# Moving left-over keys and score pairs, and holding loads to four in flight, in a T5-bias attention with a maxout feed-forward

## The chip, the cores and the metric

The kernel runs on one core of one Trainium2 chip. The metric is the device time in microseconds of one execution. One launch computes everything; nothing is computed on the host.

## What is computed

Attention with a bias that depends on the distance of query and key alone, for 8 batch elements, 8 heads, 576 positions and 64 elements a head, and behind it a feed-forward layer that takes the largest of three products:

```python
scores = scale * np.matmul(q, k.transpose(0, 1, 3, 2))
scores = scores + bias.transpose(2, 0, 1)[None, :, :, :]      # bias_table[bucket(|i - j|)]
attn = np.exp(scores - max) / sum                             # softmax over keys
attn_out = np.matmul(attn, v)
x = attn_out.transpose(0, 2, 1, 3).reshape(4608, 512)
h = np.maximum(np.maximum(x @ w1, x @ w2), x @ w3)            # 512 -> 768
out = h @ w_out                                               # 768 -> 512
```

## The kernel before

**Tiling.** A *visit* `(b, hp)` is a batch index `b` (0 to 7) and a pair of heads `hp` (0 to 3). Its 576 positions are four tiles of 128 and a rest of 64, the left-over keys and queries. Scores are computed with the keys on the partitions; ScalarE takes their exponential (`exp`, line 800) into `e4` (four key tiles) and `el` (left-over keys of both heads in its first 576 columns, left-over queries behind them). The bias is a factor: VectorE multiplies the columns near the diagonal by a band (`times_band`, `times_bandt`, `times_band_left`). `attend` or `attend_rows` multiplies by `v`, whose extra column of ones gives the sums, and its `quotients` divide into `x_sb`. After a batch's last head pair SP's DMA transposes bring `x_sb` into `xT` (lines 946, 994), which the feed-forward reads.

**Stages.** Batches 0 and 1 and visit (2,0) use small portions of the feed-forward between the attention's parts (`fill`, which also calls the *hooks* that it is given between portions). In later visits a feed-forward whose matmuls use 64 rows of the array, in pairs, takes the place of the portions: the *tiled* visits, from (2,2) on, take their feed-forward from `plain_gates` and `plain_outputs`, in the order `begin0, end0, begin1, end1`; `begin` computes the first rows' half, `end` the other half. From visit (4,0) (`ROWS`) on, scores run one key tile at a time over 512 queries (`key_scores`, two matmuls), the attend is `attend_rows`, and the next visit's first key tile is already computed by `ahead` at the end of a visit. (4,0) has no visit of this form before it, so its list `begun` is empty.

**PSUM.** Scores, left-over keys (`sct`) and left-over queries (`scq`) share the pool `ps_s` with two buffers, so each needs the exponential of the last but one to be done.

**Order.** Every engine runs its instructions in the order of the program, where `inorder` asks for it. On TensorE this is nearly everything. SP issues all DMA transposes and the output stores in one order. POOL issues the loads of `q`, `k`, `v` (they cast to bf16): from batch 2 on it does nothing else.

**Loads.** In `b`'s visit `hp == 2`, `load_v(b + 1)` is issued behind a transpose of batch `b + 1` (for `b` from 4 on, the one of the last full key tile), then `load_qk(b + 2)`. These are six transfers for v (four tiles and two tails) and eleven for q and k (eight tiles, q's tail, two of k's). `load_qk(b + 2)` goes behind the same transposes for `b < 4`, behind v's last transfer (`last_v`) from `b = 4` on. All of a batch's transposes `transposes(b + 1)`, five pairs of q and k with the tails last, are issued during visits `hp` 1 and 2 of batch `b`. A dependence of this sort is a semaphore wait on POOL, added by `go_behind`.

**Lines that the steps touch.** `in_turn` (147) wraps each load; `keys_first` (1192) sets the order of the score groups of visits (2,0) and (3,0); lines 1194 to 1200 begin a rows visit; 1245 is its third key tile; 1272 to 1284 are the tiled visit with the left-over keys of (3,0); 1323 and 1330 issue the loads; 1340 to 1344 end a visit that isn't tiled, with the left-over keys of (2,0) behind the hooks.

Of the kernel before, what the change touches and what calls it, by code (L numbers as in the profile page):

```python
# [39 lines left out]
def kernel(  # L40
# [21 lines left out]
    QM = 2 * QS  # L62
    KT = 4
    ROWS = (4, 0)
    FCH = d_ff // P
    DCH = d_model // P
    NTOK = B * S
# [76 lines left out]
    def tail_part(src, b, h0, h1, par):  # L144
        return src[b, h0 + par : h1 : 2, KT * P : S, :].rearrange("h p d -> p h d")

    def in_turn(b, load):
        return inorder(load)

    def load_main(src, b, h0, h1, dst, t0=0, t1=KT):  # L150
        x = main_part(src, b)
# [45 lines left out]
    def load_v(b, h0, h1, behind=None):  # L197
        loads = load_main(v, b, h0, h1, vx[b % 2][:, :, :, 0:D]) + load_tail(v, b, h0, h1, v_diag)
        go_behind(loads, behind)
        return loads[-1]  # L200
# [972 lines left out]
    for b, hp in [(b, hp) for b in range(1, B) for hp in range(HP)]:  # L1173
        if hp == 0:
            x_sb[b] = x_tile()
        qT, kT = (x[:, hp, :] for x in qk[b])
        e4, el = begun[0] if begun else e_tiles()
        together = b > 1 and (b, hp) != (2, 0)
        tiled = bool(stages)
        rows = (b, hp) >= ROWS  # L1180
        if (b, hp) == ROWS:
            free_banks()
            ps_a, ps_f = banks(1)
            pending.clear()
            thirds = [after]
        rate = 8 if b == 1 or (b, hp) == (2, 0) else 13

        if tiled:  # L1190
            run, after = stages.pop(0)
        keys_first = hp == 0 and b in (2, 3)
        order = [(0, 0), (1, 0), (0, 2), (1, 2)] if keys_first else [(0, 0), (0, 2), (1, 0), (1, 2)]
        if rows:
            if not begun:
                key_scores(qT, kT, e4, 0)
            begun.clear()
            end_sums = late.pop(0)()
            key_scores(qT, kT, e4, 1)
            quotients = end_sums()  # L1200
        else:
            for c, tt in order[:2]:
                scores(qT, kT, e4, c, tt)
        store_outputs()
        if b == 1:
            if hp == 0:
                crossbar = transposes(2)
            next(crossbar, None)
        elif hp and b + 1 < B:
            if hp == 1:  # L1210
                crossbar = transposes(b + 1)
            for _ in range((KT + 1, 2, KT + 1)[min(b, 4) - 2]):
                next(crossbar, None)
        early()
        if turned:
            turned.pop(0)()
        if not rows:
            quotients = next_late()
        if not tiled or rows:
            times_band(hp, e4, 0, 0, QS, inorder)  # L1220
        quotients()
        if rows:
            times_band(hp, e4, 1, 0, QM, inorder)
        if b == 1 and hp + 1 < HP:
            spread_packed(hp + 1, nc.vector)
        if (b, hp) == (1, 1):
            add_ffn(QS, QS)

        def keys():
            sums_first = together and (not tiled or len(pending) < 2)  # L1230
            if sums_first:
                next_late()()
            if (b, hp) != (3, 0):
                left_keys(hp, qT, kT, el, 0, S)
            if together and not sums_first:
                next_late()()

        if rows:
            begin2, end2 = thirds.pop()()
            if not run.keys_late:  # L1240
                end_keys = left_keys_rows(qT, kT, el)
            begin2()
            if not run.keys_late:
                end_keys()
            key_scores(qT, kT, e4, 2)
            largest = end2(2 if run.keys_late else 1)

            def bands():
                times_band(hp, e4, 2, 0, QM, inorder)
                times_bandt(hp, el)  # L1250
                times_band(hp, e4, 3, 0, QM, inorder)

            def left():
                left_queries(hp, qT, kT, el)
                times_band_left(hp, el)

            def ahead():
                n = HP * b + hp + 1
                if n < HP * B:
                    begun.append(e_tiles())  # L1260
                    key_scores(*(x[:, n % HP, :] for x in qk[n // HP]), begun[0][0], 0)

            run(
                lambda: key_scores(qT, kT, e4, 3), left, ahead, largest, bands, lambda: left_keys_rows(qT, kT, el)
            )
            thirds.append(after)
        elif tiled:
            if len(pending) > 1:
                fill(DCH)
            keys()  # L1270
            fill(FCH)
            if (b, hp) == (3, 0):
                left_keys(hp, qT, kT, el, 0, S)
            times_band(hp, e4, 0, 0, QS, inorder)
            begin0, end0, begin1, end1, alone = run
            scores(qT, kT, e4, *order[2])
            begin0()
            exp_left = left_queries(hp, qT, kT, el)
            turned_1 = begin1()
            times_band(hp, e4, 1, 0, QM, inorder)  # L1280
            band_left = times_bandt(hp, el)
            go_behind([band_left], turned_1[-1])
            times_band_left(hp, el)
            scores(qT, kT, e4, *order[3])
            dve0 = end0([exp_left])
            dve1 = end1([band_left])
            times_band(hp, e4, 2, 0, QM, inorder)
            dve0()
            times_band(hp, e4, 3, 0, QM, inorder)
            dve1()  # L1290
            pending.extend((n, [fn]) for n, fn in alone)
        else:
            late_keys = (b, hp) == (2, 0)
            fill(8 if (b, hp) == (2, 1) else rate, (lambda: None) if late_keys else keys, *([lambda: None] if together else []))
            if not late_keys:
                times_bandt(hp, el)


            def beside_scores():
                banks = [pool.tile([P, KT * 64], F32, tag=tag, name="scq") for pool, tag in ((ps_a, "a"), (ps_f, "ff"))]  # L1300
                turn_left_queries(qT, kT, banks)
                put_left_queries(el, banks)

            visit(qT, kT, e4, order[2:], None if together else beside_scores, el=el if together else None)
        store_outputs()
        if b == 1 or hp in (1, 2) and b + 1 < B:
            for _ in range(2 if b > 1 else 1):
                next(crossbar, None)
        early()
        if turned:  # L1310
            turned.pop(0)()
        if not together:
            quotients = next_late()
            times_band(hp, e4, 1, 0, QM, inorder)
            quotients()
        if b == 1 and hp + 1 < HP:
            second_transposes(qk[1], hp + 1)
        if hp == 1 and b > 1:
            pending.extend((n, [fn]) for n, fn in rest)
            rest.clear()  # L1320
            made, tail = ffn((b - 1) * CH, CH, False, [(b + (i + 2) // HP, (i + 2) % HP) >= ROWS for i in range(HP)])
        if hp == 2 and b + 1 < B:
            last_v = load_v(b + 1, 0, H, turned_qk[b + 1, 1, 1 if b < 3 else 2 if b == 3 else KT - 1])
            if b == 1:
                load_last_weights(turned_qk[2, 1, KT - 1])
                batch[3] = load_tiles()
                load_qk(3, turned_qk[2, 1, KT - 1])
        if hp == 2 and 1 < b < B - 2:
            batch[b + 2] = load_tiles()
            load_qk(b + 2, turned_qk[b + 1, 1, KT - 1] if b < 4 else last_v)  # L1330

        def queries():
            times_band(hp, e4, 3, 0, QM, inorder)

        def bands_2():
            for t in range(1 if together else 2, 3):
                times_band(hp, e4, t, 0, QM, inorder)

        if not tiled:
            fill(rate, bands_2, queries)  # L1340
            if late_keys:
                keys()
                times_bandt(hp, el)
            times_band_left(hp, el)
        if hp == 1 and b > 1:
            stages.extend(made)
            strict.append(b)
        if ROWS <= divmod(HP * b + hp + 1, HP) < (B, 0):
            late.append(lambda b=b, hp=hp, e4=e4, el=el: attend_rows(b, hp, e4, el))
            continue  # L1350
        for half in range(2):
            late.append(lambda b=b, hp=hp, e4=e4, el=el, half=half: attend(b, hp, e4, el, half))
# [50 lines left out]
```

## Time and profile before

| | us |
|---|---|
| median of 3 runs | 312.46 (311.75 to 313.81) |
| the profiled execution, whole | 312.09 |
| its span on the core | 310.3 |
| TensorE busy | 296.2 |
| ScalarE busy | 202.0 |
| VectorE busy | 206.9 |
| visits (4,0) to (7,3), about | 122 to 252 |

The page counts an engine as busy while an instruction of it is under way; the rest of its span it waited or had nothing to do. Busy shares by slice of the span, in tenths (40 slices of 7.76 us), and the share of the 16 DMA engines:

```profile
PE   8889989999998999999999999989999999999995
...
DVE  6487878777775767676777677765777665553552
ACT  3999978977767677868776877775777730122221
POOL 8977660962087104930429032832300000000000
...
DMA  9999999999999999999699999999932113202003
```

The transfers keep the DMA engines occupied until about 235 us. By queue:

```profile
q0 software_dynamic: 103840, 16.66, 78.3%
q1 hardware_dynamic: 58304, 22.69, 44.7%
q8 instruction: 35, 0.57, 0.8%
```

The columns are packets, MB and the time the packets took, as a share of 16 engines' span. `q0` are POOL's loads, `q1` what SP issues, `q8` the engines' instructions.

### The profile page before, as it was taken

How to read it: one execution, taken by the hardware profiler on the slowest of the kernel's cores; microseconds unless marked ns; L12 is line 12 of the kernel's file. 1: busy time of each engine (PE TensorE's matmuls, PEld its weight loads, DVE VectorE, ACT ScalarE, POOL GpSimd, SP SyncE). 2: the span in 40 equal slices, each digit the busy share in tenths (PEclk: the TensorE clock that was granted, in tenths of full speed). 3: DMA queues.
4: the chain of work that ended last, by engine and by line, in shares of the span. 5: the costliest groups of instructions: out<-in, count | busy, mean ns of one | idle time of the engine just before them, and what ended most of it. 6: DMA issues, size and time to landing. Idle time of an engine off the chain costs nothing.

```text
span 310.3 us, 10531 instructions
## 1 busy us (share of the span) xinstructions
PE 296.2 (95%) x4534; PEld 182.3 (59%) x4547; DVE 206.9 (67%) x471; ACT 202.0 (65%) x273; POOL 110.6 (36%) x147
## 2 busy tenths in 40 slices
PE   8889989999998999999999999989999999999995
PEld 2357867765554655667666666666667654444442
DVE  6487878777775767676777677765777665553552
ACT  3999978977767677868776877775777730122221
POOL 8977660962087104930429032832300000000000
PEclk9999999999999999999999999999999999999999
DMA  9999999999999999999699999999932113202003
GB/s 166 179 197 198 181 166 142 100 163 133 141 137 223 145 183 157 122 135 139 152 169 104 139 114 225 131 135 172 176 63 106 37 19 93 101 0 104 34 0 135
DMA packets 163950, 40.48 MB, mean 130 GB/s; under 512 B 153784, under 2 KB 159424, under 8 KB 163904
## 3 DMA queue, kind: packets, MB, share of 16 engines
q0 software_dynamic: 103840, 16.66, 78.3%
q1 hardware_dynamic: 58304, 22.69, 44.7%
q8 instruction: 35, 0.57, 0.8%
q10 hardware_dynamic: 1760, 0.47, 0.7%
q14 instruction: 11, 0.09, 0.1%
HBM read 35.39 MB, written 9.45 MB: 144 GB/s over the span
## 4 chain that ended last, share of the span: by engine, by line
PE 74%; DMA 11%; ACT 4%; SPq 4%; DVE 2%; issue 1%; POOL 0%; POOLq 0%
PE psp L107 31%; PE ps L107 15%; PE a L107 11%; PE sc L107 7%; DMA q_sb<-in_q_dram 5%; PE pso L107 5%; SPq L711 4%; ACT e L800 4%; DMA vx<-in_v_dram 2%; DMA kT<-k_sb 2%; PE sct L107 2%; DMA kT<-ktail 2%; PE warm L107 1%; PE scq L107 1%; PE tp L111 1%
## 5 line engine op out<-in xcount | busy, mean ns | idle before, releaser
L800 ACT ACTIVATE e<-sc 128x1024 bf16<-128x1024 f32 x128 | 128.8, 1026 | 29.8 <-PE sc L107 28.6
L107 PEld LDWEIGHTS <-w_bf 64*128 64x128 bf16 (+1 forms) x1088 | 73.7, 95 | 57.5 <-issue 3.4
L107 PE MATMUL psp<-xT,w_bf 64*128 64x512 bf16 x736 | 91.2, 376 | 1.4 <-DVE e L780 1.3
L780 DVE TENSOR_TENSOR e<-e,hank 128x512 bf16<-128x512 bf16 (+2 forms) x120 | 56.4, 476 | 17.6 <-ACT e L800 17.2
L107 PE MATMUL ps<-xT,w_bf 128*128 128x512 bf16 (+1 forms) x345 | 64.7, 335 | 1.4 <-DVE k_sb L228 1.0
L153 POOL DMA_DIRECT2D vx<-in_v_dram x28 | 24.6, 897 | 73.8 <-PE scq L107 26.0
L107 PE MATMUL sc<-qT,kT 64*128 64x256 bf16 (+1 forms) x384 | 47.9, 306 | 2.3 <-ACT e L800 1.0
L107 PEld LDWEIGHTS <-kT 64*128 64x128 bf16 (+1 forms) x736 | 30.6, 94 | 28.1 <-issue 8.7
L107 PE MATMUL a<-vx,e 64*128 64x65 bf16 (+1 forms) x1536 | 44.6, 191 | 0.0
L107 PEld LDWEIGHTS <-e 64*128 64x128 bf16 (+1 forms) x1536 | 40.6, 95 | 3.8
L107 PEld LDWEIGHTS <-hT 64*128 64x128 bf16 (+1 forms) x444 | 27.2, 95 | 19.2 <-DVE hT L528 1.3
L800 ACT ACTIVATE el<-sct 128x576 bf16<-128x576 f32 (+2 forms) x36 | 21.7, 606 | 16.3 <-PE sct L107 15.1
L107 PE MATMUL a<-vt,el 64*128 64x65 bf16 (+1 forms) x240 | 30.9, 201 | 0.4 <-DVE m L488 0.4
L398 ACT ACTIVATE m<-ps 128x512 bf16<-128x512 f32 x14 | 8.4, 597 | 34.3 <-PE ps L107 34.3
L107 PEld LDWEIGHTS <-el 64*128 64x128 bf16 (+1 forms) x624 | 25.9, 95 | 8.1 <-issue 5.5
L107 PE MATMUL psp<-wo_bf,hT 64*128 64x256 bf16 (+1 forms) x336 | 29.7, 307 | 0.0
L181 POOL DMA_DIRECT2D q_sb<-in_q_dram x24 | 22.2, 926 | 15.3 <-DMA xT<-x_sb 6.8
L181 POOL DMA_DIRECT2D k_sb<-in_k_dram x24 | 22.2, 924 | 3.3 <-DMA wo_bf<-in_moe_w_out_dram 1.2
L107 PE MATMUL pso<-wo_bf,hT 128*128 128x512 bf16 (+2 forms) x103 | 22.6, 367 | 0.2
L800 ACT ACTIVATE el<-scq 128x512 bf16<-128x512 f32 (+1 forms) x38 | 19.5, 530 | 2.7 <-PE scq L107 2.6
L407 DVE TENSOR_TENSOR m<-ps,m 128x512 bf16<-128x512 f32 x14 | 9.7, 692 | 17.0 <-PE ps L107 17.0
L107 PE MATMUL sct<-qT,kT 64*128 64x288 bf16 (+3 forms) x96 | 16.7, 284 | 2.9 <-DMA kT<-ktail 1.6
(83 smaller groups left out, 291.5 us busy)
## 6 DMA issues: line engine op xcount, KB each, us to landing
out_dram<-osb SPq DMA_DIRECT2D x35, 256.0 KB, 2.8
vx<-in_v_dram POOLq DMA_DIRECT2D x28, 128.0 KB, 6.6
q_sb<-in_q_dram POOLq DMA_DIRECT2D x26, 128.0 KB, 7.6
k_sb<-in_k_dram POOLq DMA_DIRECT2D x24, 128.0 KB, 8.0
w_bf<-in_moe_w_dram POOLq DMA_DIRECT2D x3, 768.0 KB, 9.3
xT<-in_k_dram SPq DMA_DIRECT2D x6, 128.0 KB, 4.3
hank<-w_dr SPq DMA_DIRECT2D x2, 384.0 KB, 5.5
wo_bf<-in_moe_w_out_dram POOLq DMA_DIRECT2D x1, 768.0 KB, 9.0
```

Source lines behind the costliest of these rows:

```text
L107: made = inorder(nc.tensor.matmul(*args, **kw))
L111: inorder(nc.tensor.transpose(*args))
L153: in_turn(b, nc.gpsimd.dma_start(out=dst[:, t, h0:h1, :], in_=x[:, t, h0:h1, :])) for t in range(t0, t1)
L181: loads.append(in_turn(b, nc.gpsimd.dma_start(out=dst[:, t], in_=main_part(src, b)[:, t])))
L398: nc.scalar.activation(out=st[fb]["m0"][:], in_=ps0, func=ACTF.Copy)
L407: inorder(nc.vector.tensor_tensor(out=m[:], in0=ps1, in1=st[fb]["m0"][:], op=ALU.max))
L711: turned_qk[b, j, t] = inorder(nc.sync.dma_start_transpose(out=made[j][:, :, P * t : P * t + n], in_=src))
L780: put(nc.vector.tensor_tensor(out=e4[:, t, :, lo:hi], in0=e4[:, t, :, lo:hi], in1=hank[:, 2 * hp : 2 * hp + 2, c0:c1][:, :, ::-1], op=ALU. ...
L800: made = nc.scalar.activation(out=out_, in_=in_, func=ACTF.Exp, scale=inv_sqrt_d)
```

## The change

Four edits, which leave the number of matmuls, activations, vector operations and transfers as it is.

1. Left-over keys. In (3,0) `left_keys` moves from ahead of the third score group to behind `begin1`. In (2,0) `keys()` and its `times_bandt` move from the end into the first hook of the last `fill`, ahead of the bands of tiles 1 to 3; and (2,0) takes its score groups in the usual order.
2. (4,0) computes the scores of key tiles 0 and 1 ahead of the attend of (3,3), and of tile 2 in its middle, where it computed tile 0 ahead, tile 1 in the middle and tile 2 after the left-over keys. The later visits, which find a begun tile, stay as they were.
3. From batch index 5 on, each load waits until the load four before it has landed. Batch 5's first four have none before them. The wait stands on POOL's queue.
4. `load_qk(b + 2)` goes behind the key transpose for all `b`, no longer behind v's last transfer: it concerns batches 6 and 7.

```diff
+    PACED, DEEP = 5, 4
...
+    in_flight = []
+
     def in_turn(b, load):
-        return inorder(load)
+        load = inorder(load)
+        if b >= PACED:
+            if len(in_flight) >= DEEP:
+                go_behind([load], in_flight[-DEEP])
+            in_flight.append(load)
+        return load
...
-        keys_first = hp == 0 and b in (2, 3)
+        keys_first = (b, hp) == (3, 0)
         order = [(0, 0), (1, 0), (0, 2), (1, 2)] if keys_first else [(0, 0), (0, 2), (1, 0), (1, 2)]
         if rows:
-            if not begun:
-                key_scores(qT, kT, e4, 0)
+            lead = not begun
             begun.clear()
+            for t in range(2) if lead else ():
+                key_scores(qT, kT, e4, t)
             end_sums = late.pop(0)()
-            key_scores(qT, kT, e4, 1)
+            key_scores(qT, kT, e4, 2 if lead else 1)
             quotients = end_sums()
...
-            key_scores(qT, kT, e4, 2)
+            if not lead:
+                key_scores(qT, kT, e4, 2)
...
-            if (b, hp) == (3, 0):
-                left_keys(hp, qT, kT, el, 0, S)
             times_band(hp, e4, 0, 0, QS, inorder)
             begin0, end0, begin1, end1, alone = run
             scores(qT, kT, e4, *order[2])
             begin0()
             exp_left = left_queries(hp, qT, kT, el)
             turned_1 = begin1()
+            if (b, hp) == (3, 0):
+                left_keys(hp, qT, kT, el, 0, S)
             times_band(hp, e4, 1, 0, QM, inorder)
             band_left = times_bandt(hp, el)
             go_behind([band_left], turned_1[-1])
...
-            last_v = load_v(b + 1, 0, H, turned_qk[b + 1, 1, 1 if b < 3 else 2 if b == 3 else KT - 1])
+            load_v(b + 1, 0, H, turned_qk[b + 1, 1, 1 if b < 3 else 2 if b == 3 else KT - 1])
...
-            load_qk(b + 2, turned_qk[b + 1, 1, KT - 1] if b < 4 else last_v)
+            load_qk(b + 2, turned_qk[b + 1, 1, KT - 1])
...
-            fill(rate, bands_2, queries)
-            if late_keys:
+            def late_products():
                 keys()
                 times_bandt(hp, el)
+
+            fill(rate, *([late_products] if late_keys else []), bands_2, queries)
             times_band_left(hp, el)
```

## The prediction

> **What bounds the kernel now.** I read the page first. TensorE has nearly every microsecond and its clock is full, so a change in other work is worth only what TensorE now loses to it.
>
> ```profile
> PE 296.2 (95%) x4534; PEld 182.3 (59%) x4547; DVE 206.9 (67%) x471; ACT 202.0 (65%) x273; POOL 110.6 (36%) x147
> PEclk9999999999999999999999999999999999999999
> ```
>
> The span is 310.3 us, so TensorE idles 14 us in all. About 6 us of that lie in the first 42 us and 3.4 us in the last 10, which the change doesn't touch. Then I asked TensorE's own timeline, from 42 us to the end, for every matmul with an idle time over 0.15 us before it. There are five; 0.31 and 0.21 us at 53.5 and 66.1 are small. The other three:
>
> ```profile
> 94.29 0.42 PE L107 MATMUL sct<-qT,kT 128*128 128x512 bf16 x2 [1.63 <-DMA kT<-ktail]
> ...
> 123.81 0.21 PE L107 MATMUL a<-vt,el 64*128 64x65 bf16 x2 [0.39 <-DVE m L488]
> ...
> 209.87 1.04 PE L107 MATMUL psp<-xT,w_bf 64*128 64x512 bf16 x8 [1.29 <-DVE e L780]
> ```
>
> The bracket is the idle time and what ended it. These 3.31 us, 1.1% of the span, are the whole purse. The chain of waits tells where the first comes from:
>
> ```profile
> 86.35 2.02 SPq L711
> ...
> 88.47 5.78 DMA kT<-ktail
> 94.25 0.05 issue
> 94.29 0.42 PE sct L107 x2
> ```
>
> SP issues batch 3's ten transposes one after the other; the last, of the left-over keys, goes out at 88.47 and lands at 94.25, 1.6 us after TensorE wants it for (3,0). The third gap is a puzzle: the VectorE product it names (208.79 to 209.21) isn't read by that matmul, and the bank it writes had last been read by a VectorE copy that ended at 207.34. The page's transfers, with the median time from issue to landing at the end, say the rest of what I use:
>
> ```profile
> vx<-in_v_dram POOLq DMA_DIRECT2D x28, 128.0 KB, 6.6
> q_sb<-in_q_dram POOLq DMA_DIRECT2D x26, 128.0 KB, 7.6
> k_sb<-in_k_dram POOLq DMA_DIRECT2D x24, 128.0 KB, 8.0
> ```
>
> POOL issues one load each 0.87 us and they take 7 to 8 us to land, so more than four are in flight: the limit will bind. That the change does nothing there is excluded.
>
> **What the skill says.** "Runtime: NRT & Kernel Launch", Instruction fetch mechanics: an engine's instructions arrive by DMA in blocks of 256, mostly hidden. The page's instruction queue agrees in size (35 packets, 0.57 MB: 16 KB each); one starts at 207.44, when TensorE had started 420 matmuls and weight loads since the last (196.65), and TensorE stands from 208.58 to 209.87. So I take the third gap for a late block; no page says that it can be that late. "DMA: Bandwidth & Descriptors", Queues, rings and completion order: an engine goes round-robin between queues, a packet at a time. The trace agrees as far as it shows: a transpose takes 2.4 us from issue to landing at best and 9.8 at worst, when loads are under way. "TensorEngine Tiling (Array Packing)", Key Properties: a change of tiling mode drains TensorE. Here eight 64-row scores would have ended about 89.18 by their mean spacing, and the 128-row product behind them starts at 89.27: an estimate of 0.09 us for a change.
>
> **The change, part by part.** The sum is against the profiled execution's own 312.09 us (span 310.3 and 1.8 around it); the median of the runs is 312.46, 0.37 above it.
>
> (3,0), left-over keys later. Nothing is removed: two matmuls (0.35 us until the next), one exponential (0.65) and one band product (0.26) go behind scores (0.23), the first rows of two gates (0.86 each) and the left-over queries (0.12). The order by TensorE from 92.66: scores, rows, queries, rows end at 94.73, and the transpose has landed at 94.25, so the 1.63 us go. The queries need q's tail, which went out two transposes earlier and landed at about 91.3. What is late next: ScalarE does this exponential third, not first, ending at 95.95, and VectorE's band product, on which the second pair's other rows wait, at 96.2, where TensorE would be at 96.15: 0.1 lost. The product now stands between 64-row matmuls: two more mode changes, 0.2. Net -1.3, bounds -1.63 and -0.5: the first attend of (3,1), 99.26 now, would run at 97.7, and batch 3's last v tail lands at 97.55, with no margin.
>
> (2,0), score order and left-over keys earlier. Same instructions. TensorE meets the keys at 64.0 instead of 64.94, their transpose landed at 63.41: no wait, 0.6 us margin. ScalarE's order is the same. VectorE is in order, though: the left-over keys' band product now stands ahead of bands 2 and 3, and waits for the exponential that ends at 66.03, where these bands started at 65.46. So they come 0.57 + 0.25 = 0.8 us later, band 2 at 66.85; attend's first half starts at 66.41 and meets it after two key tiles, at 66.5. +0.4 (0 to +0.8).
>
> (4,0), two score pairs first. The second pair (0.22 us) fills the gap of 0.39 before attend. But the scores have two banks: the third pair then needs the first one's exponential (ends 124.76, TensorE there at 124.56) and the keys behind it the second's (ends 125.8, there at 125.6). What is filled is paid back: 0 (-0.25 to +0.2).
>
> Loads from batch 5 on. The first four of q, k(5) go as before; the fifth waits for the first, and so on. POOL has no other work at that time, so behind its waits stand only loads. q and k(5) land 2.7 to 5.5 us before their transposes are issued; one waiting longer by up to 4 us costs little. For v, six loads, the last tail now waits for the second v tile: it landed 7.4 us after the first issue in batch 5, and a lone load lands in 3.7 to 4.0 us, so the last tail lands 11.4 us after the first issue in place of 10.4 (151.70 to 162.11); the same sum gives 10.9 against 11.0 in batch 6 and 11.5 against 10.0 in batch 7. Attend wants them at 163.09, 194.74 and 227.69, margins of 1.0, 0.0 and 2.6. The transfers before v(5) shift with TensorE by the 0.9 net gained so far, since xT's transposes start on VectorE's quotients and SP runs on from there: wanted 162.2, landed 162.2. Cost 0 (to +1.0).
>
> q and k(6), (7) directly behind v. They waited for all of v; SP then stood before their transposes: 165.1 to 166.16 and 168.4 to 169.91 in batch 6, 198.0 to 199.49 and 200.7 to 201.37 in batch 7. This 2.5 and 2.1 us go, and v(6), which waits for the last of these key transposes, is issued 2.5 us earlier: the margin of nothing at 194.74 becomes 2. TensorE gains what it lost there, about 0.15 (first attend group 0.91 against 0.75 us). Loads now run beside xT's transposes (158 to 165), which have over 3 us until the gates read them: 0.
>
> The fetch at 208. No more than four loads ahead of a block, and q, k(7) earlier: likely less, but it is one event in one execution. -0.65, bounds -1.29 and, if another block is caught elsewhere, +0.7.
>
> Sum: -1.3 + 0.4 + 0 + 0 - 0.15 - 0.65 = -1.7, so 310.4 on the profiled time and 310.8 on the median; I say 310.5.
>
> **The rivals.** First, *all gaps close*: -1.63 - 0.25 - 0.15 - 1.29 with (2,0) free is -3.3: 308.8. For it speaks that each gap has its own edit; against it the two-bank and band arithmetic above. Second, *the gain turns into waits for v*: TensorE gains 1.3 in batch 3 and gives it back at (3,1) and (5,0), where v lands on no margin, and the fetch gap stays: 312.1. Third, on the other side, *the limit starves v*: each last tail goes out a landing later. The price: 2.5 us later than computed at (5,0) is 2.5 lost, the chain through transposes to the next v doesn't recover, 2.5 again at (6,0) less 2.0 of margin is 0.5, fetch blocks and late transposes of batch 7 at most 1.0; with none of the gains, 312.1 + 4.0 = 316.1. It decides from the point where v's last tail lands more than 12.4 us after the first issue. Against it: the loads are issued 0.9 us apart and four cover 3.5 us of a lone load's 3.7.
>
> **How the numbers follow.** Under 1% this kernel's measurement hardly tells a change from none. My forecast, a gain between 0.3 and 1%, has 0.50, with 309.4 to 311.6 as its own range; all gaps close 0.24; gain given back 0.16; v starved 0.10. Faster by over 1% (under 309.3) is the first rival, 0.24; within 1% the forecast and the second, 0.66; slower 0.10. The range, 308.8 to 313.0, holds the forecast, the second rival with its spread of the runs shown (311.75 to 313.81), and half of the first.
>
> **What would show it.** In the changed profile: the 1.63 before sct in (3,0) gone, with at most 0.3 before the next attend; a wait of 0.3 to 0.5 at the first attend of (2,1) on VectorE's bands; at (4,0) 0.1 to 0.2 left and small waits on exponentials after it; SP without the waits before batches 6's and 7's first transposes; no idle TensorE before the attends of (5,0) and (6,0). I am wrong if a wait on vx or vt of 1 us or more appears there, if left-over keys in (2,0) wait for their transpose, or if issue gaps grow in number.

## The result: 310.77 us, and where the time went

| | before | changed |
|---|---|---|
| median of 8 runs, us | 312.79 (311.75 to 314.11) | 310.77 (308.73 to 311.51) |
| ratio, 95% interval | | 0.9919 (0.9894 to 0.9943) |
| profiled execution, us | 312.09 | 311.51 |
| span, us | 310.3 | 309.7 |

The change makes the kernel 0.8% faster, 2.0 us on the medians. Ratios, and means over profiles, compare undisturbed executions alone, so a ratio can differ a little from the quotient of two medians. The changed kernel's profile comes from its slowest execution, and 1.1 us of that arose before any edit acts: it waited 0.85 us for a copy at 31.4 and 0.41 us at 36.5, in stretches where the two programs do the same. So I compare the two traces by stretches. This is the page of the changed kernel; the source has grown by eight lines at this point, so lines are up to 8 higher (L711 is L719, L153 is L161):

```profile
PE 297.2 (96%) x4547; PEld 182.1 (59%) x4547; DVE 207.4 (67%) x471; ACT 202.0 (65%) x273; POOL 110.6 (36%) x147
...
L189 POOL DMA_DIRECT2D k_sb<-in_k_dram x24 | 21.6, 899 | 10.3 <-DMA vx<-in_v_dram 4.3
...
vx<-in_v_dram POOLq DMA_DIRECT2D x28, 128.0 KB, 6.3
q_sb<-in_q_dram POOLq DMA_DIRECT2D x26, 128.0 KB, 6.6
k_sb<-in_k_dram POOLq DMA_DIRECT2D x24, 128.0 KB, 7.5
```

Each group shows count, busy time, mean ns, then the idle time ahead and what ended most of it. POOL now waits 10.3 us ahead of k's loads, 4.3 of them for loads of v (3.3 in all before): the limit binds. Half of the loads of q land within 6.6 us of their issue, in place of 7.6. These are TensorE's idle times over 0.15 us between 68 us and its last attend, from its timeline:

```profile
123.58 0.21 PE L108 MATMUL a<-vt,el 64*128 64x65 bf16 x2 [0.17 <-DVE m L496]
...
158.74 1.90 PE L108 MATMUL psp<-xT,w_bf 64*128 64x512 bf16 x16 [0.54 <-issue]
...
189.27 0.23 PE L108 MATMUL a<-vx,el 64*128 64x65 bf16 x3 [0.41 <-issue]
```

The 1.63 us before `sct` are gone. The 0.39 of (4,0) became 0.17. The 1.29 us at 209.87 are gone, but two smaller gaps of the same sort have come in other places. The view ends them by "issue": nothing that it shows was waited for.

A finer ruler than the span is the moment at which VectorE starts a visit's quotients. Changed minus before, us, at the same point of the work:

```
after the quotients of      offset   step   what lies between
(1,3), at 61.80 before      +1.11           start, the same in both programs
(2,2), at 92.08             +1.34    +0.23  (2,0) to (2,2): the edit of (2,0)
(3,0), at 102.00            -0.23    -1.57  the edit of (3,0)
(3,3), at 125.90             0.00    +0.23  the edit of (4,0)
(4,3), at 157.22            -0.01    -0.01
(5,0), at 165.00            +0.70    +0.71  the gap at 158.74
(5,2), at 181.01            +0.39    -0.31
(5,3), at 188.84            +0.96    +0.57  the gap at 189.27 (ahead of this instruction)
(6,0), at 196.81            +0.80    -0.16
(6,2), at 213.98            -0.67    -1.47  the gap at 209.87 of before
end                         -0.59    +0.08
```

From (1,3) on that makes 1.7 us gained. It looks like the prediction's own sum, term by term, but the experiments show that two of these terms differ from one execution to the next. I call such a term a draw.

### The profile page after: what moved, and what is told of

It reads as the page before. It is cut to its first block, busy times and chain, and to the rows that moved or that the text cites. A ratio compares the mean times of both kernels' runs of the same rounds, so it can differ in the third digit from the quotient of the medians.

```text
span 309.7 us, 10546 instructions
## 1 busy us (share of the span) xinstructions
PE 297.2 (96%) x4547; PEld 182.1 (59%) x4547; DVE 207.4 (67%) x471; ACT 202.0 (65%) x273; POOL 110.6 (36%) x147
## 4 chain that ended last, share of the span: by engine, by line
PE 81%; DMA 9%; POOL 4%; ACT 2%; issue 2%; DVE 1%; POOLq 0%; ACTq 0%
PE psp L108 34%; PE ps L108 17%; PE a L108 12%; PE sc L108 8%; PE pso L108 6%; DMA w_bf<-in_moe_w_dram 5%; DMA xT<-in_k_dram 4%; PE sct L108 2%; POOL vx L291 2%; ACT e L808 1%; POOL q_sb L161 1%; PE scq L108 1%; DMA out_dram<-osb 1%; ACT el L808 0%; POOL vt L180 0%
## 5 line engine op out<-in xcount | busy, mean ns | idle before, releaser
L161 POOL DMA_DIRECT2D vx<-in_v_dram x28 | 24.7, 895 | 57.3 <-PE sc L108 33.1
L189 POOL DMA_DIRECT2D k_sb<-in_k_dram x24 | 21.6, 899 | 10.3 <-DMA vx<-in_v_dram 4.3
L536 DVE TENSOR_TENSOR hT<-psp,m 128x1024 bf16<-128x1024 f32 (+1 forms) x16 | 15.0, 956 | 7.3 <-PE psp L108 7.3
```

Source lines behind the costliest of these rows:

```text
L161: in_turn(b, nc.gpsimd.dma_start(out=dst[:, t, h0:h1, :], in_=x[:, t, h0:h1, :])) for t in range(t0, t1)
L189: loads.append(in_turn(b, nc.gpsimd.dma_start(out=dst[:, t], in_=main_part(src, b)[:, t])))
L536: inorder(nc.vector.tensor_tensor(out=out_[:, i : i + n], in0=ps2()[:, i : i + n], in1=m[0][:, i : i + n], op=ALU.max,))
```

## The experiments

Two theories stood at first. A: the moved keys of (3,0) carry most of the gain (my terms: -1.3 there, -0.65 for late instruction blocks). B: the limit of four carries it. Each part was made alone, then in twos.

**The left-over keys of (3,0) alone.**

```diff
-            if (b, hp) == (3, 0):
-                left_keys(hp, qT, kT, el, 0, S)
             times_band(hp, e4, 0, 0, QS, inorder)
...
             turned_1 = begin1()
+            if (b, hp) == (3, 0):
+                left_keys(hp, qT, kT, el, 0, S)
```

> The kernel before with the left-over keys of (3,0) moved alone. Theory A (the moved keys carry the gain): the idle 1.63 us before sct near 94 is gone, the first attend of (3,1) starts 1.3 to 1.6 us earlier beside the visits ahead of it, and the time is 1.0 to 1.6 us below before (ratio 0.995 to 0.997). Theory B (the load limit carries it, the gap only moves to a wait for v in (3,1)): within 0.4 us of before.

Measured: ratio 0.9969 (0.9943 to 0.9994), 1.0 us faster, with no change only just outside the interval. The wait is gone, the stretch gained 1.46 us against the profile of before. By itself that fits A.

**The edit of (2,0) alone.** `keys_first = (b, hp) == (3, 0)`, and `late_products` as the first hook.

> The kernel before with (2,0)'s score order and left-over keys changed alone. Theory A (VectorE's bands come late and the first attend of (2,1) meets them): 0.2 to 0.5 us slower between the last attend of batch 1 and (2,2), no wait for a transpose. Theory B (the keys are free there): no change of that stretch within 0.1 us. A wait for the left-over keys' transpose of 0.3 us or more would be against both.

Measured: ratio 1.0006 (0.9981 to 1.0032). The quotients of (2,0) come 0.54 us late, but at those of (2,1) 0.10 us are left, and no wait for a transpose is seen: nearly free. The profile shows more elsewhere:

```profile
97.95 0.22 PE L107 MATMUL a<-vt,el 128*128 128x130 bf16 x1 [0.69 <-DMA vt<-in_v_dram]
...
179.16 1.04 PE L107 MATMUL psp<-xT,w_bf 64*128 64x512 bf16 x8 [1.67 <-issue]
211.26 1.04 PE L107 MATMUL psp<-xT,w_bf 64*128 64x512 bf16 x8 [1.81 <-issue]
```

This kernel has the keys of (3,0) where they were, and yet no wait for their transpose; it waited for v's tail instead, at (3,1), and for 0.44 us in two parts at (5,0). And what stood once at 209.87 stands here twice, with 1.67 and 1.81 us. One profile's 1.63 and 1.29 were draws.

**The edit of (4,0) alone.** `lead`, key tiles 0 and 1 ahead, 2 in the middle.

> The kernel before with (4,0)'s two leading score pairs alone. Theory A (two banks: what is filled is paid back): the gap of 0.39 before the attend of (3,3) falls to about 0.17, but the quotients of (3,3) come 0 to 0.25 us later than before, beside the visits ahead. Theory B (filling the gap is a gain): they come 0.2 us earlier.

Measured: ratio 0.9999 (0.9974 to 1.0024). The gap before the attend fell from 0.39 to 0.17, and the quotients of (3,3) came 0.23 us later against those ahead. The same 0.23 appears in each of the three profiles with this edit, and 0.00 in those without. That is theory A: the two banks ask back more than was filled. In the changed kernel the third score pair starts at 124.58, behind an exponential that ends at 124.53, and the left-over keys at 125.50, behind one that ends at 125.45.

**Both load edits alone.** `PACED, DEEP = 5, 4`, `in_turn` as changed, and `load_qk` behind the key transpose.

> The kernel before with both load edits (four in flight from batch 5 on, q and k behind the key transpose) alone. Theory A (loads cost TensorE only at (6,0) and by late instruction blocks): 0 to 1.0 us faster, batch 5's transposes end 2 to 3 us earlier than before's 152.4, gaps in the middle of psp runs stay but shrink in sum from 1.3 to under 1.0 us. Theory B (this is the main gain): 1.3 us or more faster and no such gap at all. Starved v: waits on vx or vt of 1 us.

> The load edits alone, a second time, beside the next run. Ratio to before 0.987 to 0.993 as the first time (0.9891). In the profile the wait for the left-over keys at (3,0) is drawn anew: between 0 and 2 us.

Measured: 0.9891 (0.9856 to 0.9927), and again 0.9926 (0.9895 to 0.9956): 2.3 to 3.4 us. That is theory B's size. The left-over keys, here where they were, waited 0.49 and 0.60 us, and the gaps that remain after 130 us are one each:

```profile
93.32 0.42 PE L108 MATMUL sct<-qT,kT 128*128 128x512 bf16 x2 [0.49 <-DMA kT<-ktail]
...
207.26 1.04 PE L108 MATMUL psp<-xT,w_bf 64*128 64x512 bf16 x8 [0.17 <-issue]
```

```profile
93.70 0.42 PE L108 MATMUL sct<-qT,kT 128*128 128x512 bf16 x2 [0.60 <-DMA kT<-ktail]
...
208.01 1.04 PE L108 MATMUL psp<-xT,w_bf 64*128 64x512 bf16 x8 [0.51 <-issue]
```

Of the load edits' expectation, the end of batch 5's transposes was a half miss: 150.0 and 151.3 in these two, a gain of 1 to 2 us and not 2 to 3; in the changed kernel itself it was 152.7, no gain.

**Following alone, and the limit alone.**

```diff
-            load_qk(b + 2, turned_qk[b + 1, 1, KT - 1] if b < 4 else last_v)
+            load_qk(b + 2, turned_qk[b + 1, 1, KT - 1])
```

> The kernel before with q and k directly behind v alone, no limit of four. If following is what clears SP's waits: the waits of 1.0 and 1.5 us before the first transposes of batches 6 and 7 go, v(6) is issued 1.5 us or more earlier than 183.7, and the time is within 0.4 us of before. If following without a limit floods the transfers: transposes of batches 6 and 7 take longer from issue to landing (over 7 us in the middle) and v(6) is no earlier.

> The kernel before with the limit of four alone, q and k of batches 6 and 7 still behind v's last transfer. If the limit is what speeds the transposes up: batch 5's last key transpose lands near 149 in place of 152.4, but q and k of batch 6 start later than before, after v's slower end, and SP waits 1.5 us or more for them; time within 0.6 us of before, to either side. If following is what counts: batch 5's transposes end where they did.

Measured: following alone 0.9954 (0.9930 to 0.9979), the limit alone 0.9902 (0.9874 to 0.9930). The limit is the larger part, and it doesn't need the other edit: alone it left a gap of 0.65 at 157.53 and no more after 130 us, and batch 5's key transposes ended at 149.3. Both times were missed: following was to stay within 0.4 us of before and gained 1.4, the limit within 0.6 and gained 3.1. Why following alone gains is not shown.

The waits on SP go. Before, SP's timeline jumps from xT's transposes to the first of batch 6, and again to the second; the changed kernel's runs through, and so does that of following alone (167.66, 0.11 us behind xT):

```profile
162.51 2.56 SPq L994 DMA_TRANSPOSE xT<-x_sb  x2
166.16 2.16 SPq L711 DMA_TRANSPOSE qT<-q_sb  x1
169.91 1.19 SPq L711 DMA_TRANSPOSE kT<-k_sb  x1
```

```profile
162.47 2.56 SPq L1002 DMA_TRANSPOSE xT<-x_sb  x2
165.14 1.21 SPq L719 DMA_TRANSPOSE qT<-q_sb  x1
166.45 1.21 SPq L719 DMA_TRANSPOSE kT<-k_sb  x1
```

But the limit alone does the same, though its q and k still go behind v's last transfer:

```profile
157.98 6.33 SPq L1002 DMA_TRANSPOSE xT<-x_sb  x4
164.42 1.22 SPq L719 DMA_TRANSPOSE qT<-q_sb  x1
```

I had expected SP to wait 1.5 us or more there. With the limit alone v(5) starts at 146.38, 5.3 us earlier than before, and q and k behind it come in time. Nor does following alone bring v(6) forward: it was expected 1.5 us or more ahead of 183.7 and came at 186.18, in an execution that ran 2.0 us behind the profile of before at (5,0).

**The gaps that "issue" ends.** I took them for late blocks of TensorE's instructions. If they are, they stand where a block ends, whatever is computed there. Here TensorE's records (matmuls, weight loads and the 38 instructions of its sequencer) are counted from the start up to each such gap after 125 us, in the profiles whose records are complete (4547 matmuls, 4547 weight loads):

```
profile          instructions ahead (and modulo 256): gap, us
keys (3,0)       5571 (195): 0.11     6849 (193): 1.26
(2,0) edit       5571 (195): 1.67     6849 (193): 1.81
(4,0) edit       4033 (193): 0.31     4801 (193): 0.71    6849 (193): 2.00
changed          4801 (193): 0.54     6083 (195): 0.41
load edits       6849 (193): 0.17
```

All stand at 193 to 195 of 256. In profiles with 13 records missing, that of before among them, they stand at 185 to 187. To tell the place in the count from the place in the work, the kernel before was given 64 more TensorE instructions at its start:

```diff
-    on_zeros(warm[:, 0:CH], 9)
+    on_zeros(warm[:, 0:64], 41, 64)
```

> The kernel before with 41 narrow warming matmuls (64 columns) in place of the first 9 wide ones: 64 TensorE instructions more ahead of all the work. If the gaps in the middle of psp runs are late instruction blocks of 256: they stand again where 193 of 256 instructions have been counted (4801, 5569, 6849 and so on, counted from the start), so 64 instructions (about 2 us) earlier in the work than in the other runs, and none before the psp matmul of visit (6,3) that has the 1.29. If that matmul or its data is the cause: the gap stays before it, at 129 or so of 256 (193 + 64). Time: 0 to 6 us slower for the longer start.

Measured (the expectation names visit (6,3); it is (6,2), and its "129 or so" is a slip): two gaps, at 5561 and 6841 instructions, 185 of 256 with 14 records missing. That is the count of before (6841), and so 64 instructions earlier in the work. The second now stands before another operation:

```profile
176.60 0.61 PE L107 MATMUL psp<-xT,w_bf 64*128 64x512 bf16 x4 [1.76 <-issue]
...
209.67 0.39 PE L107 MATMUL sc<-qT,kT 64*128 64x512 bf16 x1 [2.67 <-issue]
```

Had the matmul's data been the cause, the count would have been 185 + 64 = 249 of 256. Ratio 1.0041 (1.0008 to 1.0074), with these larger gaps; a longer start isn't seen (first quotients at 19.39, before 19.37). So it is shown: TensorE stands at the ends of blocks, as its instructions come late. The packets of `q8` are TensorE's: 35 of 256 instructions make 8960, and TensorE has 9119 records. In the profile of before the block's packet starts at 207.44, 16 instructions ahead of the stop; the one before it (196.65) had started 180 ahead. From the packet's start to TensorE's next matmul 2.4 us pass, and at the ten gaps of the table 2.2 to 3.2. It is the start that is late.

The sum of these gaps after 125 us is, without the limit, 1.41 (before), 1.37, 3.48 and 4.43 us, mean 2.67; with the limit of four it is 0.95 (changed), 0.17, 0.65, 1.06, 0.51 and 2.13, mean 0.91. The limit takes away 1.8 us of late blocks by these means; they are of four and six profiles, and the largest sum with it is above the smallest without.

**Two loads in place of four.** `PACED, DEEP = 5, 2` in the changed kernel.

> The changed kernel with two loads in flight in place of four. A lone load takes 3.7 us, so two give one load each 1.9 us or more: v's last tail lands about 3 x 4 = 12 us and q and k's eleven about 22 us after their first issue. If v can be starved (the rival that ended slower): TensorE waits 1 us or more before the attends of (5,0) or (6,0) and the time is 1 to 4 us above the changed kernel. If there is slack: within 0.5 us of it.

Measured: ratio 1.0566 (1.0516 to 1.0616), 20 us slower than the changed kernel; the expectation's 1 to 4 us was far too small. It begins with the starved v of the prediction's third rival, and then the keys' transposes are late:

```profile
166.60 0.20 PE L108 MATMUL a<-vt,el 64*128 64x65 bf16 x1 [4.15 <-DMA vt<-in_v_dram]
...
198.19 0.42 PE L108 MATMUL sct<-qT,kT 64*128 64x288 bf16 x2 [3.98 <-DMA kT<-ktail]
...
207.71 0.54 PE L108 MATMUL a<-vt,el 64*128 64x65 bf16 x2 [1.62 <-DMA vt<-in_v_dram]
```

v(5)'s last tail lands 15.9 us after its first issue (151.69 to 167.58), past the 12.4 at which I had put the turning point; in the changed kernel it is 11.5 us (148.05 to 159.50). The turning point itself was too strict: with the load edits alone the tail took 12.44 us, and no attend waited, as the first issue had come at 148.19.

The waits from 160 us on sum to 15.3 us. The rest lies in TensorE's granted clock, here in tenths of full speed for 40 slices of 8.3 us:

```profile
PEclk9999999999999999999979998799989999999999
```

Four times the trace shows the granted clock at half for 3.41 us, from 167.17, 197.89, 208.13 and 238.85 on, each within 0.7 us of the end of one of the waits of 4.15, 3.98, 1.62 and 3.32 us. Half of four times 3.41 is 6.8 us, and TensorE is busy 6.6 us longer than in the changed kernel. All six executions had a mean granted clock of 0.979 or lower.

**The limit from batch 2 on**, with the load edits and the keys of (3,0).

> The left-over keys of (3,0) moved and the two load edits, with the limit of four from batch 2 on in place of 5. If crowded loads also make the late transposes and instruction blocks of batches 2 to 4: no gap over 0.2 us between 65 and 125 but the 0.39 before the attend of (3,3), and 0.3 to 1.0 us faster than the same with the limit from 5. If v or keys of batch 3 starve: waits of 0.5 us or more on vx, vt or kT there and no gain.

Measured: 1.0009 (0.9965 to 1.0052), against 0.9919 and 0.9916 for the same from batch 5 on: the 0.3 to 1.0 us that I expected on top didn't come, and the whole gain was lost. POOL's queue tells why. Ahead of `wo_bf` stands v(2)'s last tail, which now waits:

```profile
58.41 0.64 POOL L180 DMA_DIRECT2D vt<-in_v_dram  x1 [0.56 <-DMA vx<-in_v_dram]
62.74 0.61 POOL L180 DMA_DIRECT2D vt<-in_v_dram  x1 [3.71 <-DMA vx<-in_v_dram]
63.35 0.85 POOL L1065 DMA_DIRECT2D wo_bf<-in_moe_w_out_dram  x1
```

`wo_bf`, 768 KB, is issued at 63.35 in place of 58.93, and TensorE waits for it:

```profile
72.74 0.58 PE L108 MATMUL pso<-wo_bf,hT 128*128 128x512 bf16 x1 [4.21 <-DMA wo_bf<-in_moe_w_out_dram]
```

The output weights are wanted early in batch 2, and a limit there holds back a load that isn't under it. Five other profiles, where the limit didn't reach this load, waited for it too, but for 0.24 to 2.06 us. The long wait costs more than itself: around it the granted clock stood at half for 6.83 us (from 71.07 on), some 3.4 us of work, and 15 of this kernel's 18 executions had a mean granted clock of 0.995 or lower. From batch 5 on nothing else stands in POOL's queue.

**The load edits with the keys of (3,0), without (2,0) and (4,0).**

> The changed kernel without the edits of (2,0) and (4,0): left-over keys of (3,0) moved, and the two load edits. If these two cost what the trace says (0.2 each): 0.2 to 0.5 us faster than the changed kernel, ratio to before 0.990 to 0.993. If they bring something: slower than the changed kernel by 0.2 or more.

> The load edits with the left-over keys of (3,0) moved, a second time, beside the last run. If moving the keys brings the mean of the waits seen without it (0.7 us over six profiles): 0.3 to 1.2 us faster than the load edits alone. If their gains overlap, as the first pair said (0.9919 against 0.9891): no faster.

Measured: 0.9919 (0.9889 to 0.9950) and 0.9916 (0.9888 to 0.9944). The second ran beside the load edits alone (0.9926): 0.3 us apart in the medians, inside the intervals. So neither the gain of the moved keys on top of the limit, nor the loss of the two small edits, shows in the time. No kernel of these is clearly faster than the changed one: the limit alone (0.9902) and the load edits (0.9891, 0.9926) lie within its interval or overlap it.

**The clock.** One stretch of half clock lowers the mean granted clock of an execution to about 0.995. The kernel before had 0.995 or lower in 51 of its 161 executions beside these runs, the kernels with the limit of four from batch 5 on in 5 of 74. So the limit also makes such stretches rarer. In the executions that the ratios compare this is little: an estimate from their mean clocks gives 0.46 to 0.60 us lost by the kernel before and 0.05 to 0.44 with the limit.

## Why the prediction was right, and where two terms were not

The time (310.5 said, 310.77 measured) and the sum (-1.7) were right. The case that I held likeliest came: less than 1% faster, medians 2.0 us apart. By steps:

- **The keys of (3,0), -1.3.** The mechanism is right: the wait goes, ScalarE and VectorE keep up, and no v is late at (3,1) in the six profiles with the move. The size is that of one draw. In the six compared profiles without the move the keys waited 1.63, 0.60, 0.49, 0, 0 and 0 us. Against the mean of these stretches (1.14 us better than before's) the moved ones (1.55) gain 0.4; the time of this edit alone says 1.0, with an interval of 0.2 to 1.8. The predicted cost of the move, 0.1 for the band product and 0.2 for the tiling modes, is borne out as a sum: stretches that had no wait at all reach -1.81, the moved ones -1.57. A slip is in the start that it gives for the attend of (3,1): 97.7 leaves out the 0.2 for the modes.
- **The fetch at 208, -0.65.** The reading as a late instruction block was right and is now shown. The size was too small: I took it for one event of 1.29 us, of which half would go. Without the limit there are 1.4 to 4.4 us of them in each profile, and the limit removes 1.8 on average. This is the term of the sum that failed most. The keys' term failed to the other side, and so the sum held: with the means in place of the draws, -0.4 for the keys, -1.8 for the blocks, 0.1 for (2,0) and 0.23 for (4,0) make -1.9. That two wrong sizes cancel is luck.
- **(2,0), +0.4.** Bands 2 and 3 came late as computed: by 0.78 us against the first attend of (2,1) (bands at 67.28 and attend at 67.45, before 65.46 and 66.41). TensorE lost 0.1 us, for band 2 begins at query 128, so the attend's first query tile doesn't read it; that I overlooked.
- **(4,0), 0.** It costs 0.23 in all three profiles with it, just over the upper bound of 0.2. The waits on two exponentials that I computed are there and outweigh what the gap gave.
- **Loads, 0.** v's last tail lands 11.45, 11.39 and 11.01 us after its first issue (said: 11.4, 10.9, 11.5), and the attends of (5,0) to (7,0) don't wait. v(5) starts 3.65 us earlier than before (148.05), not 0.9, as the transpose of batch 5's last full key tile lands sooner.
- **q and k behind v, -0.15.** SP's waits go as said, but they go with the limit alone too. The 0.15 us at (6,0) had nothing to do with it: every other profile but that with two loads, with or without the edit, has this stretch 0.16 to 0.20 us shorter than the profile of before.

Of the rivals, "the gain turns into waits for v" was seen once, 0.69 us at (3,1), in a kernel that hadn't moved the keys. "v starves" is real at a limit of two and absent at four. "All gaps close" (308.8 us) came close in the load edits' first run, whose profiled execution took 309.48 us. No rival had the clock in it, which made about a third of the loss at a limit of two.

What stays open: why the start of a block's packet is late. That fewer loads in flight make it less late is shown; whether its request waits in the DMA engines' queues behind loads, or elsewhere, no view here tells. Nearly all of the gain in the compared profiles is of this kind: the stretch from (4,3) to the end is 2.3 us shorter with the limit (means of six and four profiles), and the gaps in this stretch make 1.95 of that. But the times gain 3.1 us with the limit alone; the clock can be a small part of the rest, and what remains is open. Open too is what decides that a wait is followed by half clock: waits of 2.67 and 1.81 us passed without it.

## What to carry to other kernels

An idle time that ends on a transfer, in one profile, can be a draw: before it is priced, look at the same point in other profiles, or price its mean. Where TensorE stands and nothing that it reads was late, count its instructions modulo 256: a constant remainder tells late instruction blocks, and here fewer loads in flight made them shorter. A limit on loads in flight is worth trying where loads crowd other transfers, but two was ruinous where four was good, and every transfer behind a waiting load on that queue waits with it. After a long wait of TensorE, read the granted clock: the wait may have cost more than its length.

## What the runs showed of the hardware

- TensorE's instructions came so late that it stood up to 2.67 us at a block's end, at 193 to 195 of 256 instructions in the profiles with complete records. The block's packet had started 2.2 to 3.2 us before the next matmul.
- Next to single waits of TensorE of 1.62 to 4.21 us its granted clock fell to half for 3.41 or 6.83 us (two loads, limit from batch 2); waits up to 2.67 us passed without that.
- The wait for one transposed tile lay between 0 and 1.63 us in the six compared profiles without the move; the executions of the kernel before spread over 2.4 us in its first 8 runs.
- With POOL held to four loads, q's median landing fell from 7.6 to 6.6 us. v's last transfer in batch 5 landed 11.45 us after the first issue in place of 10.4, but at 159.50 in place of 162.11, as the first issue came 3.65 us earlier.
